# An inverse transform on half-height PE tiles, and a new written-out order, in a two-layer kernel on one core

## The chip, the cores and the metric

The kernel runs on one core of a Trainium2 chip. A core has TensorE (PE, matmuls, writes to PSUM), VectorE (DVE), ScalarE (ACT), GpSimd (POOL) and SyncE (SP, which here only issues DMAs), each with its own instruction queue, worked off in order; they meet through semaphores. The metric is the device time of one execution in microseconds, the median of several runs.

## The reference

The sequence has 2,048 positions of 512 channels, bf16. Two layers, each a mixer and an MLP, and each preceded by a layer norm:

```python
k_shift = sum of four taps of k over time     # a short filter per channel
kv  = k_shift * v
y   = irfft(rfft(kv, 4096) * rfft(ssm_k, 4096))[:2048] + kv * ssm_D
x   = x + layernorm(x) * y                    # q of the mixer is the normed x
h   = gelu(layernorm(layernorm(x)) @ w1 + b1) # 512 -> 1376
x   = x + h @ w2 + b2                         # 1376 -> 512
```

`y` depends on k, v and the filter alone, not on x: it is computed once and used by both layers. The norm before the MLP is followed by the MLP's own, so it is taken twice in a row. The long convolution (`y`) and the two MLPs are nearly all of the work.

## The kernel before, in words

The sequence is treated in two halves of 1,024 positions (half 0, half 1), each transformed by a two-step Fourier transform written as matmuls:

- `turn`, `shift_turn`: transposes of the filter `ssm_k` and of k on PE. `shift`, `shift_pair`: the four-tap filter as matmuls, `shift` with 64-row tiles (line 610), `shift_pair` with 32-row tiles (line 638); VectorE multiplies by v (lines 616 and 647).
- `stage1` (line 553, tags h1 for the filter and x1 for kv): 128 points, on PE tiles of 128 rows by 64 columns.
- `stage2` (line 565, tags h2, x2): eight points by the table S2, 16 matmuls of 64 columns to a tile. The result has channels, frequencies and real or imaginary part mixed over the partitions.
- `swap`: DMAs from SBUF to SBUF that exchange real and imaginary rows, so that VectorE can multiply the two spectra (line 464).
- `inverse1` (line 665, tags i1_0 and i1_1) and `inverse2` (line 683, i2_0, i2_1): back again. `inverse1` works on eight tiles `j` of eight channel groups `i`; each has two matmuls `n` (two addends) with the spectrum as weights, read at a stride of four elements, and 128 columns of the table U. All of a spectrum must be there before its first tile. `evac` (lines 469 on ScalarE and 470 on VectorE) takes the tile out of PSUM.

The products of half 1 are formed by the multiplies of tag x2_1 and the adds of tag sum (VectorE, lines 777 and 779); i1_1 reads them.

Around this run the MLPs: 13 blocks of 128 to 512 positions, nine of half 0 (both layers) and four of half 1. A block is statistics and norms on VectorE, GpSimd (the power for the reciprocal root) and ScalarE, a transposing DMA (line 866), the matmuls m1 (line 886) with gelu on ScalarE (line 891), and m2 (line 920), cut in pieces of 4, 4 and 3 matmuls of 512 columns, with the residual add on VectorE (line 924). Blocks of half 0 fill PE while half 1 is transformed.

The order is written out by hand of a planner: all 1,185 operations are numbered as the program text makes them, and `SEQ` lists the numbers. Each engine's queue is the sublist that falls to it. `ENGS` chooses the engine of every operation that has a choice (a, v, p for ACT, DVE, POOL), `BANKS` the PSUM bank of every tile. Waits follow from the data. Numbers that matter here: 4 to 7 loads of the filter, 8 to 11 of k, 12 to 15 of v, 16 to 31 of S2, 133 to 136 of the filter's second half, 195 to 198 of q; 356 to 371 i1_1 (even a PE tile, odd its eviction), 372 to 385 i2_1; 682, 735 to 737 and 739 pieces of m2; 898 on, the first block of half 1.

```python
o.eng = o.engs[0] if len(o.engs) == 1 else {"a": ACT, "v": DVE, "p": POOL}[next(choice)]
```

Of the kernel before, what the change touches and what calls it, by code (L numbers as in the profile page):

```python
# [36 lines left out]
class Prog:  # L37
# [60 lines left out]
    ENGS = ("apvpvvvpavaavaaaaaavvvaaavvvpvpvaavaaaaavaavvaaaaaaaavavaaaaaavaaavaaaaaappppaaaaaaaaaaaaaaaaaaaaaaaaaaaaapvvp"  # L98
            "paappvppaappvvvpaappaappaappaappaappaappvavpaappvappaappvvppvvvpaappvvavvvvvvavpvvvvppavavpvvvvvpvaaavpvvaaapv"
            "avva")  # L100
    BANKS = ("02220326464004602026041320002442462264542202240064064646402046462667062260046446220462640604660406064226644472"
             "44450442172316353547502206314500451400554567076567013226140174645320543403764701436154766316307007062272260403"
# [243 lines left out]
def _tables():  # L346
# [10 lines left out]
    S2 = np.zeros((2, 8, 8, 128, 2, 8, 8))  # L357
# [603 lines left out]
```

## Time and profile before

| | |
|---|---|
| median of 3 runs | 239.22 us (239.12 to 239.52) |
| span of the profiled execution | 238.6 us; its time with what lies around the span is not listed apart |
| PE busy | 226.9 us, 95% |
| VectorE busy | 178.1 us, 75% |
| ScalarE busy | 159.6 us, 67% |
| GpSimd busy | 55.3 us, 23% |
| mean granted PE clock | 0.993 |
| moved by DMA | 26.75 MB, most of it before 60 us |

In a row of the profile, L665 is line 665 of the kernel. A group's row gives shapes, the count, after the bar the busy time and the mean duration of one in ns, and then the engine's idle time just before them with what ended it. Matmuls overlap in the pipe: their durations (some 219 ns for 128 columns) are much longer than the distance between two starts, so costs on PE are read from starts. The timeline merges neighbours of one kind and shows the start, the length and the count.

### The profile page before, as it was taken

What the parts mean: (1) busy time and instruction counts of PE and PEld (TensorE: products, weight loads), DVE (VectorE), ACT (ScalarE), POOL (GpSimd) and SP (SyncE); (2) the same over time, 40 slices, a digit from 0 to 9 for tenths busy, and PEclk for the clock granted to TensorE, in tenths of its full rate; (3) what the DMA queues carried; (4) which work ended last, traced back from release to release, by engine and by line L of the source; (5) the groups of instructions that cost most, each with busy time, mean ns of one, the idle gap of its engine ahead of it and who ended that gap; (6) DMA issues with size and microseconds to landing.
All of it is one profiled execution on the core that took longest, in us unless ns stands there. A gap on an engine that the chain in (4) does not pass through costs nothing.

```text
span 238.6 us, 6251 instructions
## 1 busy us (share of the span) xinstructions
PE 226.9 (95%) x2615; PEld 152.3 (64%) x2637; DVE 178.1 (75%) x358; ACT 159.6 (67%) x255; POOL 55.3 (23%) x120
## 2 busy tenths in 40 slices
PE   6998698899999999999999999999999999999995
PEld 3897588885968588667769675644445444444454
DVE  0579869999999999999999999593579469404013
ACT  2586879999996899999768786359036606831630
POOL 2421030104623506446004522303020210200000
PEclk9999979999999999999999999999999999999999
DMA  6999767989946660053100304200300050132202
GB/s 173 350 393 388 272 181 186 257 267 194 163 87 197 153 140 3 1 69 103 54 0 15 80 0 83 49 3 12 78 0 3 18 157 0 25 66 91 84 0 91
DMA packets 41112, 26.75 MB, mean 112 GB/s; under 512 B 23702, under 2 KB 33788, under 8 KB 41084
## 3 DMA queue, kind: packets, MB, share of 16 engines
q1 hardware_dynamic: 40786, 26.20, 40.5%
q8 instruction: 21, 0.34, 0.6%
q10 hardware_dynamic: 298, 0.16, 0.3%
q14 instruction: 7, 0.06, 0.1%
HBM read 15.07 MB, written 2.10 MB: 72 GB/s over the span
## 4 chain that ended last, share of the span: by engine, by line
PE 83%; DVE 6%; DMA 4%; ACT 3%; issue 2%; POOL 1%; SPq 1%; POOLq 0%
PE ps L886 32%; PE ps L920 31%; PE ps L665 6%; PE ps L553 5%; PE ps L565 3%; ACT ar L469 3%; DMA ar<-in_A_ssm_k_dram 2%; DVE ar L464 2%; DMA ar<-ar 2%; DVE ar L616 1%; PE ps L683 1%; PE ps L909 1%; PE ps L638 1%; PE ps L610 1%; DVE ar L470 1%
## 5 line engine op out<-in xcount | busy, mean ns | idle before, releaser
L891 ACT ACTIVATE ar<-ps,sm 128x256 bf16<-128x256 f32 (+4 forms) x143 | 65.4, 525 | 41.0 <-PE ps L886 39.5
L469 ACT ACTIVATE ar<-ps 128x1024 bf16<-128x1024 f32 (+3 forms) x77 | 71.3, 1005 | 16.4 <-PE ps L553 6.4
L886 PE MATMUL ps<-ar 128*128 128x256 bf16 (+4 forms) x568 | 81.5, 297 | 0.3
L920 PE MATMUL ps<-ar 128*128 128x512 bf16 (+1 forms) x324 | 77.2, 379 | 1.1 <-issue 0.3
L886 PEld LDWEIGHTS ps<-ar 128*128 128x128 bf16 (+1 forms) x572 | 52.8, 100 | 28.1 <-ACT ar L891 0.4
L464 DVE TENSOR_TENSOR ar<-ar 128x512 bf16<-128x512 bf16 (+3 forms) x105 | 62.7, 637 | 0.9 <-ACT ar L469 0.4
L920 PEld LDWEIGHTS ps<-ar 128*128 128x128 bf16 (+1 forms) x341 | 32.4, 98 | 33.4 <-ACT ar L891 0.2
L924 DVE TENSOR_TENSOR ar<-ar,ps 128x512 bf16<-128x512 bf16 x31 | 20.7, 678 | 33.2 <-PE ps L920 33.0
L797 DVE BATCH_NORM_STATS2 sm<-ar 128x6 f32<-128x512 bf16 x64 | 42.9, 683 | 0.5
L822 ACT ACTIVATE ar<-ar,sm 128x512 bf16<-128x512 bf16 x34 | 26.4, 811 | 9.5 <-DVE sm L809 8.3
L804 POOL TENSOR_TENSOR sm<-sm 128x2 f32<-128x2 f32 (+2 forms) x26 | 23.6, 909 | 23.8 <-DVE sm L802 22.0
L802 POOL TENSOR_SCALAR sm<-sm 128x2 f32<-128x2 f32 (+2 forms) x21 | 6.4, 304 | 97.3 <-DVE sm L798 97.1
L553 PE MATMUL ps<-ar 128*64 128x128 bf16 x512 | 18.6, 227 | 3.1 <-issue 1.4
L565 PEld LDWEIGHTS ps<-ar 128*128 128x128 bf16 x512 | 18.4, 102 | 3.4 <-ACT ar L469 1.0
L565 PE MATMUL ps<-ar 128*128 128x64 bf16 x512 | 19.6, 199 | 0.5 <-ACT ar L469 0.4
L553 PEld LDWEIGHTS ps<-ar 128*64 128x64 bf16 x512 | 15.7, 114 | 6.1 <-issue 2.6
L812 POOL TENSOR_SCALAR sm<-sm 128x1 f32<-128x1 f32 x43 | 16.1, 390 | 2.0
L470 DVE CAST ar<-ps 128x1024 bf16<-128x1024 f32 x11 | 13.3, 1222 | 4.3 <-PE ps L565 2.8
L665 PE MATMUL ps<-ar 128*128 128x128 bf16 x256 | 15.0, 219 | 0.5 <-DVE ar L464 0.4
L665 PEld LDWEIGHTS ps<-ar 128*128 128x128 bf16 x256 | 14.7, 113 | 1.2 <-DVE ar L464 0.6
L823 DVE TENSOR_SCALAR ar<-ar,sm 128x512 bf16<-128x512 bf16 x30 | 11.8, 410 | 3.4 <-POOL sm L812 3.1
L470 DVE COPY ar<-ps 128x1024 bf16<-128x1024 bf16 (+1 forms) x9 | 5.5, 632 | 8.0 <-PE ps L516 5.3
(41 smaller groups left out, 94.3 us busy)
## 6 DMA issues: line engine op xcount, KB each, us to landing
ar<-tab_s SPq DMA_DIRECT2D x16, 256.0 KB, 9.0
ar<-ar SPq DMA_DIRECT2D x16, 256.0 KB, 3.7
ar<-in_A_ssm_k_dram SPq DMA_DIRECT2D x8, 256.0 KB, 6.8
ar<-in_A_q_dram SPq DMA_DIRECT2D x8, 256.0 KB, 4.7
ar<-in_A_v_dram SPq DMA_DIRECT2D x8, 256.0 KB, 6.1
out_dram<-ar SPq DMA_DIRECT2D x7, 256.0 KB, 2.5
ar<-in_B_w_dram SPq DMA_DIRECT2D x4, 344.0 KB, 4.8
ar<-in_B_w_dram SPq DMA_DIRECT2D x5, 256.0 KB, 4.0
```

Source lines behind the costliest of these rows:

```text
L464: return P.op(eng, lambda e: e.tensor_tensor(o, a, b, op), dur, reads=[a, b] + list(more), writes=[o])
L469: return e.activation(dst, src(), AF.Copy)
L470: return e.tensor_copy(dst, src())
L553: r = e.matmul(Q(tl, 64 * ri, 64, i * 128, [1, 128]), w, m, start=True, stop=True)
L565: r = e.matmul(Q(tl, 0, 128, i // 8 * 512 + i % 8 * 4, [32, 16], [1, 4]), w, m, start=True, stop=True)
L665: r = e.matmul(Q(tl, 0, 128, i * 128, [1, 128]), w, m, start=n == 0, stop=n == 1)
L797: P.op(DVE, lambda e, sj=sj, x=x: e.bn_stats(sj, x), 600.0, reads=[x], writes=[sj])
L804: P.op(POOL, lambda e: e.tensor_tensor(r, v, hf, ALU.pow), 420.0 + 149.0 * n, reads=[v, hf], writes=[r])
L822: return e.activation(o, x, AF.Identity, bias=u, scale=r)
L886: r = e.matmul(Q(tl, 0, rows, 0, [1, w]), a, m, start=dk == 0, stop=dk == 3)
L891: P.op(ACT, lambda e, dst=dst, tl=tl, rows=rows, bias=bias, w=w: e.activation(dst, Q(tl, 0, rows, 0, [1, w]), AF.Gelu_apprx_tanh, bias=bia ...
L920: r = e.matmul(Q(tl, 0, 128, 0, [1, 512]), ins[fc][0], ins[fc][1], start=fc == 0, stop=fc == 10)
```

## The change

The output columns of S2 change places: channel `d` of a group of eight moves from the middle of the partition index to its front, even channels first. So partitions 0 to 63 hold the even channels of a group and 64 to 127 the odd ones. The rows of U follow. For half 1 `inverse1` uses this: in place of a matmul over 128 rows and 128 columns it issues two, one on rows 0 to 63 for the even channels and one on rows 64 to 127 for the odd ones, each with 64 columns of U at a step of two elements, the two into different PSUM banks. The eviction then writes with a step of two. i1_0 stays as it is.

Further, `SEQ`, `ENGS` and `BANKS` are replaced as a whole. Of the operations with a choice, 32 go to VectorE from elsewhere and 26 leave it. On PE, i1_1 was one tile, three matmuls of m2 and then seven tiles; it is now four tiles, seven matmuls of m2, four tiles. All eight of its evictions are on ScalarE in both.

```diff
     SEQ = (
-        33, 34, 6, 214, 1, 44, 0, 35, 36, 4, 7, 2, 39, 51, 3, 38, 11, 52, 8, 41, 9, 10, 45, 5, 195, 15, 12, 54, 46, 13, 53,
...
-        766, 800, 723, 802, 764, 730, 717, 731, 857, 858, 679, 685, 724, 862, 803, 718, 861, 859, 713, 714, 681, 686, 366,
-        722, 682, 732, 368, 863, 804, 367, 805, 864, 865, 866, 364, 806, 369, 360, 767, 809, 365, 810, 361, 358, 359, 765,
-        356, 357, 362, 370, 807, 811, 735, 808, 363, 812, 371, 683, 867, 813, 736, 374, 372, 737, 373, 873, 376, 868, 738,
...
+        42, 0, 6, 43, 214, 1, 4, 33, 2, 5, 34, 41, 7, 3, 195, 9, 11, 10, 8, 196, 51, 14, 197, 45, 52, 12, 209, 46, 35,
...
+        731, 343, 681, 732, 751, 684, 355, 720, 754, 685, 752, 799, 686, 755, 368, 753, 800, 687, 358, 369, 757, 360,
+        359, 801, 366, 855, 756, 735, 367, 802, 758, 856, 803, 804, 682, 361, 759, 370, 760, 862, 761, 356, 762, 371,
+        858, 364, 857, 763, 860, 357, 362, 805, 766, 736, 806, 363, 767, 861, 764, 863, 859, 739, 807, 365, 864, 808,
...
-    S2 = S2.transpose(0, 1, 2, 3, 5, 6, 4).reshape(128, 128 * 128)
+    S2 = S2[..., [0, 2, 4, 6, 1, 3, 5, 7]].transpose(0, 1, 2, 3, 6, 5, 4).reshape(128, 128 * 128)
...
-    U = U.transpose(1, 2, 0, 3, 4, 5, 6).reshape(128, 256)
+    U = U[:, :, [0, 2, 4, 6, 1, 3, 5, 7]].transpose(2, 1, 0, 3, 4, 5, 6).reshape(128, 256)
...
-    def inverse1(p, q, Z):
+    def inverse1(p, q, Z, split):
...
-                    ins.append((i, n, A(0, 128, r + (dg // 4) * 512 + dg % 4, [4, 128]), A(0, 128, R_U + n * 128, [1, 128])))
+                    o = r + (dg // 4) * 512 + dg % 4
+                    if split:
+                        for g in range(2):
+                            ins.append((512 * g + 4 * i, n, A(64 * g, 64, o, [4, 128]), A(64 * g, 64, R_U + n * 128 + g, [8, 16], [2, 4])))
+                    else:
+                        ins.append((i * 128, n, A(0, 128, o, [4, 128]), A(0, 128, R_U + n * 128, [1, 128])))
...
-                    r = e.matmul(Q(tl, 0, 128, i * 128, [1, 128]), w, m, start=n == 0, stop=n == 1)
+                    r = e.matmul(Q(tl, 0, 128, i, *([32, 16], [1, 4]) if split else ([1, 128],)), w, m, start=n == 0, stop=n == 1)
                 return r
-            P.op(PE, f, 16 * 56.0, reads=[x for y in ins for x in y[2:]], tile=tl)
+            P.op(PE, f, 32 * 18.0 if split else 16 * 56.0, reads=[x for y in ins for x in y[2:]], tile=tl)
+            if split:
+                evac(BOTH, A(0, 128, Z + 64 * j, [1, 2], [512, 16], [2, 32]),
+                     lambda tl=tl: Q(tl, 0, 128, 0, [512, 2], [32, 16], [1, 32]), E1, tl)
+                continue
...
-    inverse1(R_1, R_2, R_3)
+    inverse1(R_1, R_2, R_3, False)
...
-    inverse1(HH, HI, R_Z1)
+    inverse1(HH, HI, R_Z1, True)
```

More of the change, by code (lines that the diff above doesn't have):

```diff
@@ L44 @@
     SEQ = (
[53 rows of a table removed]
[L98 to L102, printed above, removed]
-             "71655156407602371631706316706615043246755274432051240747516203416017010")
[55 rows of a table added]
+    ENGS = (
+            "avapapvpaavvaavaavaaaaavvvvapvppvavvavaavaavvaaaaaaaavaaaaaaaaavaavaaaaaapvpvaaaaaaaaaaaaaaaaaaaaaaaaaaa"
+            "aappappaavpvppaappvvppaapvaappaappaappaappaappavppvappaapvaappvvppvappvapvvvaapvavavvvvavvvvvvvvpvvvvvvv"
+            "aavvpvaavvvvavvv")
+    BANKS = (
+            "45704306202464200000627236026646246464226006402420624644066042640262264660244620204426464644246204266020"
+            "22247020226337626301520172570440464475725755436672367720371021321620440063513741720454430362521124671007"
+            "27743140661373223714364027332203342000120556367705202105351567170234501404453107474")
     def __init__(self, nc):
```

100 rows, old and new, of the table SEQ are left out of this document.

## The prediction

> **What bounds the kernel now.** I read the page's busy shares first.
>
> ```profile
> span 238.6 us, 6251 instructions
> ...
> PE 226.9 (95%) x2615; PEld 152.3 (64%) x2637; DVE 178.1 (75%) x358; ACT 159.6 (67%) x255; POOL 55.3 (23%) x120
> ```
>
> TensorE (PE) is the bound, but a share of the span mixes stages. So the second view is the busy time in stretches: after each stretch stand its length, then PE, weight load (PEld), DVE, ACT, POOL, granted clock, DMA share and GB/s.
>
> ```profile
> 60.00:125.00 65.00, 64.18 (x909) 48.38 (x920) 64.40 (x112) 56.62 (x113) 24.14 (x41) 1.00 0.41 89
> 125.00:147.00 22.00, 21.89 (x218) 15.99 (x218) 21.23 (x59) 17.80 (x27) 8.51 (x19) 1.00 0.17 38
> 147.00:236.00 89.00, 88.53 (x448) 43.93 (x454) 46.17 (x113) 39.28 (x66) 9.48 (x20) 1.00 0.17 44
> ```
>
> From 60 us to the end PE hardly stops: 174.60 of 176 us. There a microsecond less of PE work is a microsecond of the result, provided that what PE waits for keeps up. What can fail to is VectorE (DVE): from 60 to 125 us it too is busy, 64.40 of 65.
>
> The changed stage is the second half's first inverse: line 665 on PE, line 469 its evictions. Third come the chain of waits in order of time (start, length) and the timelines of PE, ScalarE and VectorE.
>
> ```profile
> 124.95 0.90 PE ps L665 x16
> ...
> 126.49 6.26 PE ps L665 x112
> ```
> ```profile
> 124.78 1.06 PE L665 MATMUL ps<-ar 128*128 128x128 bf16 x16
> ```
> ```profile
> 127.43 6.52 ACT L469 ACTIVATE ar<-ps 128x1024 bf16<-128x1024 f32 x7 [0.52 <-PE ps L665]
> ```
> ```profile
> 111.96 12.78 DVE L464 TENSOR_TENSOR ar<-ar 128x2048 bf16<-128x2048 bf16 x14
> ```
>
> The stage starts on PE at 124.78, as VectorE ends the sums that it reads (111.96 + 12.78 = 124.74). Two busy engines meet there with no slack.
>
> **The change, part by part.** *PE work of i1_1.* Removed are 128 matmuls, 0.90 + 6.26 = 7.16 us, 55.9 ns each. Added are 256 matmuls of 64 rows and 64 columns, in 128 pairs of an upper and a lower row tile. The rows that bound the price of a pair, from PE's timeline, the chain and the groups by shape:
>
> ```profile
> 15.76 2.82 PE L610 MATMUL ps<-ar 64*128 64x256 bf16 x66
> ...
> 20.16 1.05 PE L610 MATMUL ps<-ar 64*128 64x256 bf16 x22
> ```
> ```profile
> 105.01 0.47 PE ps L565 x16
> ```
> ```profile
> 72.05 1.11 PE L638 MATMUL ps<-ar 32*128 32x128 bf16 x88
> 73.10 4.54 PE L886 MATMUL ps<-ar 128*128 128x256 bf16 x40
> ```
> ```profile
> L886 PEld LDWEIGHTS ps<-ar 128*128 128x128 bf16 x520 | 47.4, 98 | 26.1 <-ACT ar L891 0.4 <-ACT ar L469 0.3
> ...
> L665 PEld LDWEIGHTS ps<-ar 128*128 128x128 bf16 x256 | 14.7, 113 | 1.2 <-DVE ar L464 0.6 <-issue 0.2
> ```
>
> Line 610 runs 64-row tiles already: 44 more matmuls take 2.82 - 1.05 = 1.77 us, 40.2 ns each, though they stream 186 columns on average (22 matmuls of one filter stream 4,096, counted in the code). At line 665's 55.9 ns for 128, 186 columns take 81 ns alone, so the two halves run side by side. A full matmul with 64 columns takes 0.47 / 16 = 29.2 ns (line 565, unit-stride weights). That is a pair's low end: 128 x 29.2 = 3.74 us. The new weights are read at a stride of four elements, as line 665's are now, and such a load lasts 113 ns against 98 for unit stride, 15 ns more. Since a unit-stride load hides within 29.2, a strided one needs at most about 44: 128 x 44 = 5.63 us. I take the middle, 36.6, as neither row is nearer: 4.68 us, a gain of **2.48** (1.53 to 3.42).
>
> A rule speaks against this. The Trainium skill, "TensorE: Matmul & The Clock Gate", section "Wait — 56ns, not 53.3ns?", says that start-to-start never drops below about 25 ns, however few the columns. Held for every matmul, it gives 256 x 25 = 6.4 us and a gain of 0.76 instead of 2.48, an estimate from that page. The trace does not agree where neighbours are on different row tiles: line 638 issues 88 between 72.05 and 73.10, 11.9 ns each.
>
> *Mode changes.* The work around i1_1 uses the whole array. PE's timeline around a column-tiled stage shows what a change of tiling costs:
>
> ```profile
> 87.54 0.64 PE L553 MATMUL ps<-ar 128*64 128x128 bf16 x16
> 88.11 2.79 PE L886 MATMUL ps<-ar 128*128 128x256 bf16 x24
> 90.83 1.53 PE L553 MATMUL ps<-ar 128*64 128x128 bf16 x48
> 92.29 2.38 PE L886 MATMUL ps<-ar 128*96 128x256 bf16 x20
> ```
>
> From start to next start, 16 take 0.57 us and 48 take 1.46: 27.8 ns each and 0.125 left over for the change back. I take 0.1 per change, for either direction. Counted in the two orders from the first MLP tile on, there are 11 changes before and 17 after: four more from i1_1, which comes in two groups of four tiles, two from x1_1, cut into more pieces. **+0.6** (0.4 to 0.75).
>
> *Evictions of i1_1.* Still eight, all on ScalarE, 6.52 / 7 = 0.93 us each; their write is now strided by two elements. Line 469's minimum, median and maximum, over evictions of many layouts:
>
> ```profile
> L469 ACT ACTIVATE ar<-ps x77: 575/1023/1166, 7.2 to 144.3; 128x1024 bf16<-128x1024 f32 x67, 128x1024 bf16<-128x1024 bf16 x4, 128x512 bf16<-128x512 f32 x4, 128x512 bf16<-128x512 bf16 x2
> ```
>
> The layout hardly shows, so I take 0. The cover: from the first i1_1 to the first i2_1 the new order gives PE 4.68 + 0.4 + five pieces of m2 (18 matmuls of 512 columns; at four times line 665's 55.9 or less, up to 4.0), some 9.0 us; ScalarE needs one tile of 0.6 and 8 x 0.93, so 8.0. An eviction may slow by 0.12 us before PE waits; past that, all eight count.
>
> *Tables.* The same bytes in another column order; stage 2 and i1_0 keep their shapes: 0.
>
> *The order, late.* Up to the last sum VectorE's new list has two more evictions of 1024 elements, two fewer transpose copies, two fewer multiplies and one norm fewer (both 512 wide, priced alike), one residual add more. Its timeline and the groups by shape price them:
>
> ```profile
> 10.46 2.35 DVE L470 CAST ar<-ps 128x1024 bf16<-128x1024 f32 x2 [1.15 <-PE ps L553]
> 13.07 1.29 DVE L470 COPY ar<-ps 128x1024 bf16<-128x1024 bf16 x2 [0.25 <-PE ps L536]
> ```
> ```profile
> L464 DVE TENSOR_TENSOR ar<-ar 128x512 bf16<-128x512 bf16 x64 | 25.2, 417 | 0.8 <-ACT ar L469 0.4
> ...
> L924 DVE TENSOR_TENSOR ar<-ar,ps 128x512 bf16<-128x512 bf16 x31 | 20.7, 678 | 33.2 <-PE ps L920 33.0
> ```
>
> With busy time over count (0.39 and 0.67) that is 2.35 - 1.29 - 3 x 0.39 + 0.67 = +0.56 us, ahead of a stage that VectorE releases. PE brings 0.2 of its own by then (x1_1's two mode changes), so up to 0.4 of waiting is new; VectorE's 0.6 us of idle between 60 and 125 may take it all. **+0.2** (0 to 0.4).
>
> Behind the sums comes the second half's first MLP block. Now VectorE's last norm for it and PE's arrival stand here:
>
> ```profile
> 146.94 0.39 DVE L823 TENSOR_SCALAR ar<-ar,sm 128x512 bf16<-128x512 bf16 x1
> ```
> ```profile
> 152.54 10.54 PE L886 MATMUL ps<-ar 128*128 128x256 bf16 x55
> ```
>
> VectorE's last norm ends 22.6 us after its last sum; its new list there is longer by about 1.9 (two multiplies, three statistics of some 0.67, aggregates, less one add): 24.5. The transposing load behind it takes about 3, so 27.5. PE reaches the block now 29.1 us after i1_1's start (152.54 and three last 256-wide tiles, 1.3), in the new order 29.1 - 2.48 + 0.4 + two more tiles of the half before, 0.9: 27.9. The wait is 0 by 0.4 us.
>
> *The order, early.* All four loads of the filter now lead, three of q come early, and the last load of v moves from the 13th place to the 17th on SyncE's queue. SyncE's timeline, the landing times of v, the stretch that gives the load rate, and v's first reader:
>
> ```profile
> 5.72 2.47 SPq L449 DMA_DIRECT2D ar<-in_A_v_dram  x4
> ```
> ```profile
> DMA to landing us min/median/max: 3.5/6.1/7.4
> ```
> ```profile
> 10.00:20.00 10.00, 9.56 (x244) 8.74 (x238) 7.76 (x10) 6.75 (x8) 1.87 (x5) 1.00 1.05 391
> ```
> ```profile
> 17.74 2.36 DVE L616 TENSOR_TENSOR ar<-ps,ar 128x1024 bf16<-128x1024 f32 x2 [1.53 <-PE ps L610]
> ```
>
> Four places of 256 KB at 391 GB/s are 2.7 us. The last v lands by 5.72 + 2.47 + 7.4 = 15.6 and its reader starts at 17.74, released by PE: 2.1 us of cover for 2.7, and VectorE has 0.9 us more other work queued ahead of that reader. I take **0**, between +2.3 and -2.5 (rivals two and three).
>
> **Sum:** -2.48 + 0.6 + 0.2 + 0 = -1.7 us, a span of 236.9. The profiled span of 238.6 lies 0.6 under the median run of 239.22, which holds what is around it; carried over: **237.5 us**.
>
> **Rivals.** *One, slower: the pace is per matmul.* If each 64-row matmul keeps line 565's 29.2 ns, i1_1 takes 256 x 29.2 = 7.48: 239.22 + 0.32 + 0.8 = 240.3. It decides above 25 ns per matmul (0.8 back from 7.16). Line 638's 11.9 speaks against it. *Two, slower: PE falls to half clock once more, early.* PE was idle before such a stretch:
>
> ```profile
> 28.20 1.42 issue
> ```
> ```profile
> 30.52 4.52 PE L565 MATMUL ps<-ar 128*128 128x64 bf16 x96
> ```
>
> 96 at 29.2 ns are 2.80 us; they took 4.52. The new order runs all of h1_0 ahead of the filters, so near 18 to 22 us PE has little but x1_0, and each of its tiles waits for a multiply of 1.18 us (line 616). One more such stretch costs 1.7, with the 0.6 by which v lacks cover 2.3: 239.8. It decides above 1.7. *Three, faster: the present stretch and stall vanish,* and the swap behind them starts earlier: 1.4 + 1.7 = 3.1 at most, some 2.5 kept: 235.0. *Four: the edit does not do what it says,* the two halves' strided loads take turns: 128 x 88 = 11.3 us in place of 7.16, 244.2. Line 638's pace speaks against it. *Five: the block behind i1_1 waits for VectorE's longer list* and the saving is given back: 239.2, for a slip of 2.1 us.
>
> **Chances.** Forecast 0.55 (its own range 236.4 to 238.8, by the ends above), two 0.20, three 0.15, one 0.05, four 0.03, five 0.02. A difference under 0.2% (0.5 us) can't be told from none. Faster is the forecast but for 0.01, and three: 0.69. Slower is one, four and 0.16 of two: 0.24. Within is the rest, 0.07. For 8 in 10 the range takes in two and three: 235.0 to 240.3.
>
> **What would show it.** Pairs of line 665's new form about 36 ns apart are right, 29 or 44 a size off, 58 or 88 rivals one and four. Further: i1_1 in two groups of some 2.4 us with changes of 0.1 around them, evictions still at 0.93, PE without gaps after 60 us, the first MLP tile near 60 us as now. It is wrong if that tile moves by over 1 us, if the clock dips a second time, or if PE waits for VectorE at i1_1 by over 0.5 us.

## The result, and the profile after

The changed kernel takes 240.13 us (median; 238.77 to 242.25), the kernel before, run beside it, 239.26: a ratio of 1.004, interval 1.0022 to 1.0058. It is slower by 0.4%, where 237.5 us and "faster" was forecast.

The head of the page of the changed kernel, and its busy time in stretches (columns as in the prediction: length, PE, PEld, DVE, ACT, POOL, granted clock, DMA share, GB/s):

```profile
span 238.0 us, 6496 instructions
...
PE 222.9 (94%) x2743; PEld 146.8 (62%) x2765; DVE 179.0 (75%) x364; ACT 161.2 (68%) x254; POOL 49.0 (21%) x104
```
```profile
60.00:125.00 65.00, 64.16 (x908) 47.17 (x917) 64.14 (x110) 55.84 (x112) 15.26 (x33) 1.00 0.43 91
125.00:147.00 22.00, 20.48 (x347) 13.62 (x345) 19.32 (x56) 21.14 (x29) 7.89 (x17) 1.00 0.13 26
147.00:236.00 89.00, 88.05 (x444) 43.62 (x450) 48.34 (x122) 37.22 (x63) 6.94 (x9) 1.00 0.20 47
```

PE's busy time fell by 4.0 us (226.9 to 222.9), 1.1 of which the profile of before owed to a stretch at half clock (below; label k, without it, has 225.8). The span hardly followed. In the stretch of the changed stage, 125 to 147 us, PE now waits 1.5 us and ScalarE is the busier engine, 21.14 of 22. The chain of waits there, PE's timeline and ScalarE's:

```profile
121.81 3.02 PE ps L933 x14
124.83 0.67 PE ps L674 x28
125.51 0.02 issue
125.53 9.59 ACT ar L473 x8
```
```profile
124.76 1.79 PE L674 MATMUL ps<-ar 64*128 64x64 bf16 x96
126.93 0.72 PE L674 MATMUL ps<-ar 64*128 64x64 bf16 x32 [0.38 <-ACT ar L473]
...
131.67 0.72 PE L674 MATMUL ps<-ar 64*128 64x64 bf16 x32 [0.47 <-ACT ar L473]
...
135.16 1.47 PE L696 MATMUL ps<-ar 128*128 128x512 bf16 x6 [0.29 <-ACT ar L473]
```
```profile
125.53 9.58 ACT L473 ACTIVATE ar<-ps 128x1024 bf16<-128x1024 f32 x8 [1.66 <-PE ps L674]
```

The chain, which was PE alone here, leaves PE after the first tile and runs through all eight evictions: 9.58 / 8 = 1.20 us each, 0.93 before. PE waits at the fourth tile, at the last, and at the second inverse. That is one place where the gain went.

The other lies ahead. Here are the largest waits of PE up to 60 us, and rows of its timeline there (start, length):

```profile
PE ps L511 <- POOL ar L505: 1.8, 1, 1.8
PE ps L614 <- DVE ar L620: 1.3, 1, 1.3
PE ps L569 <- ACT ar L473: 1.1, 3, 0.5
PE ps L557 <- POOL ar L468: 1.1, 1, 1.1
PE ps L557 <- ACT ar L473: 1.0, 1, 1.0
PE ps L887 <- ACT ar L835: 0.8, 1, 0.8
```
```profile
11.34 1.98 PE L557 MATMUL ps<-ar 128*64 128x128 bf16 x64 [1.07 <-POOL ar L468]
...
19.85 1.05 PE L614 MATMUL ps<-ar 64*128 64x256 bf16 x22 [1.33 <-DVE ar L620]
...
59.15 0.84 PE L899 MATMUL ps<-ar 128*128 128x128 bf16 x12 [0.22 <-ACT ar L473]
59.85 0.40 PE L887 MATMUL ps<-ar 128*128 128x128 bf16 x4
60.11 3.94 PE L899 MATMUL ps<-ar 128*128 128x128 bf16 x60
63.89 0.63 PE L569 MATMUL ps<-ar 128*128 128x64 bf16 x16
```

The first wait is the start of PE's work, 1.3 us in the kernel before. At 11.34 PE waits for a one-row add of the filter's transpose (line 468 on GpSimd); on GpSimd's queue two filter tables (line 527, 0.65 us each) stand ahead of it. At 19.85 the last 64-row filter tile waits for a multiply of VectorE (line 620). For comparison, the kernel before in a run without half clock, the same places and the two ends of the part behind (label k below; lines 553, 565, 610, 886, 665 and 909 are 557, 569, 614, 899, 674 and 922 after):

```profile
19.18 1.08 PE L553 MATMUL ps<-ar 128*64 128x128 bf16 x32 [0.43 <-DVE ar L616]
20.32 1.05 PE L610 MATMUL ps<-ar 64*128 64x256 bf16 x22
...
29.66 3.23 PE L565 MATMUL ps<-ar 128*128 128x64 bf16 x96
...
58.38 3.97 PE L886 MATMUL ps<-ar 128*128 128x128 bf16 x68
62.18 0.63 PE L565 MATMUL ps<-ar 128*128 128x64 bf16 x16
...
122.77 1.06 PE L665 MATMUL ps<-ar 128*128 128x128 bf16 x16
...
232.18 1.99 PE L909 MATMUL ps<-ar 128*128 128x256 bf16 x22
```

Before, tiles of another stage (line 553) fill PE ahead of the last filter tile. i1_1 starts at 122.77 there, at 124.76 in the changed kernel: 2.0 us lost ahead of the stage that was to bring the gain.

### The profile page after: what moved, and what is told of

The parts are those of the page before. It is cut to its first block, busy times and chain, and to the rows that moved or that the text cites. A ratio compares the mean times of both kernels' runs of the same rounds, so it can differ in the third digit from the quotient of the medians.

```text
span 238.0 us, 6496 instructions
## 1 busy us (share of the span) xinstructions
PE 222.9 (94%) x2743; PEld 146.8 (62%) x2765; DVE 179.0 (75%) x364; ACT 161.2 (68%) x254; POOL 49.0 (21%) x104
## 4 chain that ended last, share of the span: by engine, by line
PE 76%; ACT 11%; DVE 7%; issue 3%; POOL 1%; POOLq 0%
PE ps L899 31%; PE ps L933 29%; ACT ar L473 9%; PE ps L569 4%; DVE ar L468 4%; PE ps L557 3%; PE ps L696 2%; DVE ar L474 2%; PE ps L614 2%; DVE ar L620 2%; PE ps L674 1%; PE ps L511 1%; ACT ar L904 1%; PE ps L922 1%; PE ps L642 1%
## 5 line engine op out<-in xcount | busy, mean ns | idle before, releaser
L904 ACT ACTIVATE ar<-ps,sm 128x256 bf16<-128x256 f32 (+5 forms) x143 | 65.8, 523 | 37.3 <-PE ps L899 37.1
L473 ACT ACTIVATE ar<-ps 128x1024 bf16<-128x1024 f32 (+3 forms) x77 | 73.8, 1038 | 14.0 <-PE ps L557 5.5
L899 PE MATMUL ps<-ar 128*128 128x256 bf16 (+5 forms) x568 | 81.9, 297 | 0.5 <-ACT ar L473 0.2
L817 POOL TENSOR_TENSOR sm<-sm 128x2 f32<-128x2 f32 (+2 forms) x26 | 21.4, 822 | 32.3 <-DVE sm L815 30.5
L569 PEld LDWEIGHTS ps<-ar 128*128 128x128 bf16 x512 | 16.6, 98 | 3.6 <-ACT ar L473 1.5
L474 DVE CAST ar<-ps 128x1024 bf16<-128x1024 f32 x13 | 15.8, 1219 | 2.4 <-PE ps L569 1.5
L674 PE MATMUL ps<-ar 64*128 64x64 bf16 (+1 forms) x384 | 12.8, 203 | 1.2 <-ACT ar L473 1.1
L674 PEld LDWEIGHTS ps<-ar 64*128 64x128 bf16 (+1 forms) x384 | 11.9, 114 | 2.8 <-ACT ar L473 2.0
L767 DVE SCALAR_TENSOR_TENSOR ar<-ar,sm,ps 128x512 bf16<-128x512 bf16 x16 | 10.7, 741 | 0.4 <-PE ps L569 0.4
L811 DVE BATCH_NORM_AGGREGATE sm<-sm 128x2 f32<-128x6 f32 x64 | 10.1, 171 | 0.6
```

What stands on the lines that cost most here:

```text
L473: return e.activation(dst, src(), AF.Copy)
L474: return e.tensor_copy(dst, src())
L569: r = e.matmul(Q(tl, 0, 128, i // 8 * 512 + i % 8 * 4, [32, 16], [1, 4]), w, m, start=True, stop=True)
L674: r = e.matmul(Q(tl, 0, 128, i, *([32, 16], [1, 4]) if split else ([1, 128],)), w, m, start=n == 0, stop=n == 1)
L817: P.op(POOL, lambda e: e.tensor_tensor(r, v, hf, ALU.pow), 420.0 + 149.0 * n, reads=[v, hf], writes=[r])
L899: r = e.matmul(Q(tl, 0, rows, 0, [1, w]), a, m, start=dk == 0, stop=dk == 3)
```

## The experiments

i1_1 cuts the kernel in two: its first matmul, and the time from there to the last matmul of the kernel, both from PE's timeline. The second number is steady to some hundredths of a microsecond; the first carries the arrival of loads and the clock of that run. The kernel before was run beside each of the others, with medians of 238.74 to 239.26 us; the ratios are to those, so times of different rows are best compared by them. "Rows" is the edit with 64-row tiles, "step" its eviction writing at a step of two.

| kernel | order | i1_1 | first i1_1 (us) | i1_1 to last matmul (us) | time (us) | ratio to before (interval) |
|---|---|---|---|---|---|---|
| before (k, l) | before | full array | 122.77, 122.80 | 111.40 | 238.37, 238.49 (one run each) | |
| after | new | rows, step | 124.76 | 110.78 | 240.13 | 1.0040 (1.0022 to 1.0058) |
| a | before | full array | 124.41 | 111.40 | 239.39 | 1.0014 (0.9988 to 1.0039) |
| b | before | rows, step | 124.02 | 112.53 | 241.19 | 1.0108 (1.0068 to 1.0149) |
| c | new | full array | 125.85 | 111.39 | 241.30 | 1.0109 (1.0070 to 1.0148) |
| d | new | rows, plain write, PSUM step | 124.67 | 112.75 | 242.93 | 1.0185 (1.0151 to 1.0218) |
| e | new | rows, plain write, banks in turns | 124.68 | 109.36 | 238.26 | 0.9986 (0.9956 to 1.0015) |
| g | before | as e | 124.41 | 110.64 | 238.53 | 0.9990 (0.9965 to 1.0014) |
| h | before, then new | as after | 128.81 | 110.75 | 244.78 | 1.0253 (1.0208 to 1.0298) |
| i | new, then before | full array | 125.61 | 111.40 | 240.82 | 1.0080 (1.0048 to 1.0112) |
| j | before, then new | as e | 133.92 | 109.34 | 247.82 | 1.0365 (1.0320 to 1.0411) |
| m | before, moved at i1_1 | as e | 123.26 | 115.28 | 243.05 | 1.0173 (1.0124 to 1.0222) |

**The edit and the order apart (a, b, c).** a is the kernel before itself. b is the changed kernel with the lists of before:

```diff
     SEQ = (
-        42, 0, 6, 43, 214, 1, 4, 33, 2, 5, 34, 41, 7, 3, 195, 9, 11, 10, 8, 196, 51, 14, 197, 45, 52, 12, 209, 46, 35,
+        33, 34, 6, 214, 1, 44, 0, 35, 36, 4, 7, 2, 39, 51, 3, 38, 11, 52, 8, 41, 9, 10, 45, 5, 195, 15, 12, 54, 46, 13, 53,
...
```

c is the new order without the edit of i1_1:

```diff
-    inverse1(HH, HI, R_Z1, True)
+    inverse1(HH, HI, R_Z1, False)
```

> The kernel before, unchanged, against itself: what a second profile of it shows. The one profile of it so far had a clock of 0.993 and a stretch at half clock near 31 us; the changed kernel's runs show 1.0. If that stretch is a feature of the order, it is there again (clock about 0.993, span 238 to 239). If it is an accident of one run, the clock is 1.0 and the span 237 to 238, about 1 us less, and the base of my sum was an untypical run. Ratio of the times 0.998 to 1.002.

> The edit alone: parity tables and the split first inverse, with the order, engines and banks of before. Theory one (the strided eviction: 9.59 us for eight on ScalarE, 1.20 each, in place of 0.93, sets the stage): i1_1 takes PE some 4.3 us instead of 7.16, but eight evictions need 9.6, the first i2_1 comes later than before by 0.5 to 1 us, PE waits 1.5 to 3 us there, and the time is within 0.5 us of before or up to 1 us over it. Rival (the new order is to blame, the edit is good): faster than before by 1.5 to 2.5 us.

> The order alone: order, engines, banks and tables of the changed kernel, i1_1 unsplit (128 rows, 128 columns, eviction in runs of eight elements as before). Theory one: evictions are back at 0.93 us, PE does 2.9 us more in i1_1 but loses the 1.5 us of waiting and 0.4 of mode changes there, so about 1 us slower than the changed kernel, 240.5 to 241.5. Rival (the order is to blame): the same or slower than that as well, so this run does not decide between them alone; with the run of the edit alone it gives the order's own cost: under theory one over 1 us against before, under the rival too. If it is faster than the changed kernel, the split as such loses.

Against itself the kernel before came out even. Either part alone costs 1.1%; together they cost 0.4%. PE's timeline of b at i1_1:

```profile
127.62 0.72 PE L670 MATMUL ps<-ar 64*128 64x64 bf16 x32 [0.20 <-ACT ar L469]
128.79 0.71 PE L670 MATMUL ps<-ar 64*128 64x64 bf16 x32 [0.45 <-ACT ar L469]
129.98 0.72 PE L670 MATMUL ps<-ar 64*128 64x64 bf16 x32 [0.48 <-ACT ar L469]
...
134.66 1.04 PE L692 MATMUL ps<-ar 128*128 128x512 bf16 x4 [0.41 <-ACT ar L469]
```

In the order of before the tiles follow one another with no other work between. Their starts then lie 1.17 to 1.19 us apart, the length of an eviction: the faster matmuls only lengthen the wait. From i1_1 on b needs 112.53 - 111.40 = 1.1 us more than before. The run is slower by more, 2.2 us by the medians, which is more than either expectation; 1.25 us of it stand in its profile ahead of i1_1 (124.02 against 122.77, same lists), as a later table load and longer "issue" waits of PE. Whether they belong to that run or to the longer program stays open.

c shows where the order costs. From i1_1 on it needs 111.39 us, the kernel before 111.40: nothing is lost or won there. Its whole loss lies ahead of i1_1, at 125.85. That is 1.1 us later than in the three other profiles of this order (124.67 to 124.76), so c's 1.1% overstates the order's own cost. And c beside the changed kernel says that even with its slow evictions the edit pays in the new order, 111.39 - 110.78 = 0.6 us, because the new order puts m2 between the tiles.

**Is it the step of two in the eviction's write? (d, e)** Both write whole runs. d writes the parities as two runs of 32 and lets the second inverse put them in place as it writes PSUM:

```diff
-                evac(BOTH, A(0, 128, Z + 64 * j, [1, 2], [512, 16], [2, 32]),
+                evac(BOTH, A(0, 128, Z + 64 * j, [32, 2], [512, 16], [1, 32]),
...
-                    r = e.matmul(Q(tl, 0, 128, al * 512, [1, 512]), a, m, start=ri == 0, stop=ri == 1)
+                    r = e.matmul(Q(tl, 0, 128, al * 512, *([64, 8], [1, 2], [2, 32]) if split else ([1, 512],)), a, m, start=ri == 0, stop=ri == 1)
```

e writes runs of 64 and reads PSUM in turns from the two banks instead:

```diff
-                evac(BOTH, A(0, 128, Z + 64 * j, [1, 2], [512, 16], [2, 32]),
-                     lambda tl=tl: Q(tl, 0, 128, 0, [512, 2], [32, 16], [1, 32]), E1, tl)
+                evac(BOTH, A(0, 128, Z + 64 * j, [512, 16], [1, 64]),
+                     lambda tl=tl: Q(tl, 0, 128, 0, [32, 16], [1, 32], [512, 2]), E1, tl)
```

> The changed kernel with the step of two moved out of the eviction: ScalarE writes even and odd channels in two runs of 32, and the second inverse of this half sorts them where PE writes PSUM (a step of two floats). Theory one: evictions of i1_1 fall from 1.20 to about 0.93 us, the stage from the first i1_1 to the first i2_1 from 10.4 to about 8.8 us, PE's waits there from 1.5 to under 0.3, and the time by 1 to 2 us against the changed kernel: 238.1 to 239.1. It falls short if PE's write at a step of two is slow: the 30 matmuls of i2_1 then last more than 216 ns from start to start. Rival (strided writes are not what costs; ScalarE is slow there for another reason, such as PSUM banks shared with PE): evictions stay at 1.15 or more and the time within 0.4 us of the changed kernel.

> The changed kernel, but each eviction of the second half's first inverse writes runs of 64 channels and takes the parities apart on the reading side (PSUM read in turns from two banks). Theory one (it is the step of two in the bfloat16 write that made the eviction 1.20 us instead of 0.93): evictions of 0.90 to 0.97 us, the stage from its first matmul to the second inverse 8.2 to 8.6 us instead of 10.40, the second inverse at 216 ns a matmul, and the run 1.5 to 2.1 us below the changed kernel: 238.0 to 238.6, ratio to before 0.995 to 0.998. Rival (reading two banks in turns costs what the write cost): evictions of about 1.2 us and a ratio of 1.004 as the changed kernel has. Third (the block behind is bound by VectorE or ScalarE): evictions 0.93, but the first matmul of the 512-wide part of the block 29.2 to 29.8 us after the stage's start as before, ratio 1.002 to 1.004.

d, ScalarE's timeline and then PE's:

```profile
125.43 3.78 ACT L473 ACTIVATE ar<-ps 128x1024 bf16<-128x1024 f32 x4 [1.66 <-PE ps L674]
129.53 3.78 ACT L473 ACTIVATE ar<-ps 128x1024 bf16<-128x1024 f32 x4 [0.33 <-PE ps L674]
```
```profile
128.78 2.56 PE L674 MATMUL ps<-ar 64*128 64x64 bf16 x128
...
133.66 2.74 PE L696 MATMUL ps<-ar 128*128 128x512 bf16 x6
```

The evictions are back at 3.78 / 4 = 0.945 us and PE no longer waits at the tiles: the step in the write was the cause. But now six matmuls of the second inverse last 2.74 us where they took 1.47 in the changed kernel, 0.21 us more each, and d is the slowest of the whole orders. e has the first without the second; ScalarE's timeline and PE's:

```profile
125.45 3.78 ACT L473 ACTIVATE ar<-ps 128x1024 bf16<-128x1024 f32 x4 [1.66 <-PE ps L674]
129.56 3.78 ACT L473 ACTIVATE ar<-ps 128x1024 bf16<-128x1024 f32 x4 [0.34 <-PE ps L674]
```
```profile
124.68 2.57 PE L674 MATMUL ps<-ar 64*128 64x64 bf16 x128
127.18 1.69 PE L933 MATMUL ps<-ar 128*128 128x512 bf16 x7
128.80 2.56 PE L674 MATMUL ps<-ar 64*128 64x64 bf16 x128
131.29 2.55 PE L933 MATMUL ps<-ar 128*128 128x512 bf16 x11
133.69 1.46 PE L696 MATMUL ps<-ar 128*128 128x512 bf16 x6
...
232.06 1.98 PE L922 MATMUL ps<-ar 128*128 128x256 bf16 x22
```

Two groups of four tiles, 2.50 us each from their start to that of the next work (127.18 - 124.68), with m2 between and no wait marked. The stage takes 9.0 us (133.69 - 124.68) and not the 8.2 to 8.6 expected: PE's own work fills it now. From i1_1 on e needs 109.36 us: 1.4 less than the changed kernel and 2.0 less than c. The run is 1.9 us below the changed kernel by the medians, 1.3 by the ratios. Against the kernel before it is even: 0.9986, an interval on both sides of 1.

**The same eviction in the order of before (g).**

b's lists and e's eviction together.

> The kernel before with its order, engines and banks, the row-tile matmuls, and the eviction that reads the banks in turns. Theory one (edit good, eviction bad): the stage to the second inverse is bound by eight evictions of 0.93 us behind a first tile of 0.53 to 0.58: 8.2 to 8.6 us instead of 9.53 before, so 0.9 to 1.3 us faster than before, ratio 0.9945 to 0.9965. Rival (the evictions cost 1.2 us on the reading side too): as the edit on the old order measured, ratio 1.011. Third (the gain is taken back behind the stage): ratio 0.998 to 1.002.

```profile
125.82 2.56 PE L674 MATMUL ps<-ar 64*128 64x64 bf16 x128
128.57 0.72 PE L674 MATMUL ps<-ar 64*128 64x64 bf16 x32 [0.19 <-ACT ar L473]
129.49 0.72 PE L674 MATMUL ps<-ar 64*128 64x64 bf16 x32 [0.20 <-ACT ar L473]
130.41 0.72 PE L674 MATMUL ps<-ar 64*128 64x64 bf16 x32 [0.20 <-ACT ar L473]
```

In PE's timeline of g the tiles now come 0.92 us apart, bound by the evictions still. From i1_1 on that is 111.40 - 110.64 = 0.8 us better than before, a little under what was expected. The run, 0.999, can't be told from none and so lies where the third theory put it, but not for its reason: the stage itself gains 0.8 (8.75 us, 133.16 - 124.41, for 9.52 in k, 132.29 - 122.77), and nothing of that is given back behind it. What hides it lies ahead of i1_1, 124.41 against 122.77 in k. In the new order the same edit is worth 2.0 (c to e), since the cover between its tiles lets PE's whole gain through.

**Where ahead of i1_1 (k, l, h, i).** k and l are the kernel before, for profiles without half clock. h has the first 314 operations (to the first MLP tile) in the order of before and goes on in the new one; i is the counterpart, 308 new ones and then the order of before, with full-array matmuls in i1_1. The joint of h against the order of before, and that of i against the new one:

```diff
-        259, 481, 484, 204, 485, 487, 486, 403, 410, 445, 411, 488,
+        259, 481, 484, 204, 485, 487, 486, 403, 302, 301, 294, 208,
```
```diff
-        401, 441, 243, 284, 442, 402, 291, 244, 257, 584, 403, 585,
+        401, 441, 243, 284, 442, 402, 291, 244, 213, 387, 443, 257,
...
-    inverse1(HH, HI, R_Z1, True)
+    inverse1(HH, HI, R_Z1, False)
```

> The kernel before once more, for a profile at the full granted clock. Theory one (the new order loses ahead of the second half's first inverse): at full clock the inverse starts at 122.9 to 123.7 us, against 124.7 to 125.9 in the four profiles of the new order. Rival (no loss there): 124.3 us or later.

> The same as the look before it, a second draw: the clock fell to half for a stretch in about half of the runs of this order. Theory one at full clock: start of the second half's first inverse at 122.9 to 123.7 us; at half clock for a stretch up to 1.5 us later. Rival: 124.3 us or later at full clock.

> The counterpart: the first 308 operations in the new order, the rest in the order of before, with full-array matmuls in the second half's first inverse (new tables and layouts). Theory one (loss in the early part): ratio 1.004 to 1.006. Rival (early part even): ratio 0.999 to 1.001.

> The changed kernel, but up to the first matmul of the first block's first layer (the first 314 operations) the order, engines and banks of before. Theory one (the new order loses 1.0 to 1.4 us in its first 60 us): 1.0 to 1.4 us below the changed kernel, ratio 0.998 to 1.000. Rival (the loss of the new order lies in the stretch from the first block to the second half's first inverse, 65.6 us instead of 64.4): ratio 1.003 to 1.005, as the changed kernel.

k and l start i1_1 at 122.77 and 122.80, 0.1 below theory one's bounds and far from the rival's. i points the same way: 111.40 from i1_1 on, exactly before's, and its start at 125.61 carries all of its 0.8%. That is more than either expectation, and i is no clean counterpart: 0.8 us of it is a wait of PE for a load of weights (in_B_w) at 69.05, behind the joint, which no whole order has.

h told nothing on the question and met neither expectation. Behind the joint PE stands for 2.5 us on VectorE, a wait that neither whole order has:

```profile
PE ps L899 <- DVE ar L767: 2.5, 1, 2.5
```

One more thing differs by the early order. The row of the granted clock in the page's 40 slices, first the kernel before in run a, then the changed kernel:

```profile
PEclk9689999999999999999999999999999999999999
```
```profile
PEclk9999999999999999999999999999999999999999
```

Of the nine profiles whose first part is in the order of before, six have such a stretch (before, a, g, h, j, m; not b, k, l), at changing places; of the five in the new order (after, c, d, e, i) none has. The mean clocks on record for single runs say the same less sharply: they are below 0.999 in 34 of 64 runs of the kernel before, and in 6 of 44 in the new order (after, c, d, e). In the kernel before the median of those 34 runs is 239.19 us, that of the other 30 is 238.55: some 0.6 us. Its profile in the prediction began i1_1 2.0 us later than k (124.78); 1.3 of that are the 96 matmuls in 4.52 us where k has 3.23, and 1.1 a longer "issue" wait just ahead of them (1.42 against 0.34), which the clock is not shown to have caused; k loses 0.4 in other places. What sets the stretch off is open.

**A better version? (j, m)** j joins the orders later, after 690 operations at about 105 us, with e's eviction. m keeps the order of before and moves work at i1_1 only:

```diff
-        679, 685, 724, 862, 803, 718, 861, 859, 713, 714, 681, 686, 366, 722, 682, 732, 368, 863, 804, 367, 805, 864,
-        865, 866, 364, 806, 369, 360, 767, 809, 365, 810, 361, 358, 359, 765, 356, 357, 362, 370, 807, 811, 735, 808,
-        363, 812, 371, 683, 867, 813, 736, 374, 372, 737, 373, 873, 376, 868, 738, 814, 869, 870, 375, 774, 385, 815,
+        679, 685, 724, 862, 803, 718, 861, 859, 713, 714, 681, 686, 366, 722, 368, 687, 367, 682, 732, 863, 804, 805,
+        364, 369, 360, 864, 865, 866, 806, 358, 683, 735, 767, 365, 809, 356, 361, 810, 765, 362, 359, 807, 736, 811,
+        370, 357, 808, 737, 363, 812, 371, 738, 813, 867, 374, 372, 373, 873, 376, 868, 814, 869, 870, 375, 774, 385,
```

In j the joint reads, where the order of before went on with 662, 733, 799, 672:

```diff
-        677, 664, 633, 665, 674, 801, 760, 726, 662, 733, 799, 672,
+        677, 664, 633, 665, 674, 801, 760, 726, 675, 672, 673, 678,
```

> The first 690 operations (to about 105 us) in the order of before, the rest in the new order, with the row-tile matmuls and the evictions that read the banks in turns. Theory one (the new order loses its 1 to 2 us ahead of the second half's first inverse and nothing behind it, and its interleaving of that inverse with the block is what makes the row tiles pay): from the inverse's first matmul to the last matmul 109.4 us, as in the changed kernel with the same evictions, behind the first part of before: 236.6 to 237.6, ratio 0.990 to 0.996. Rival (a junction of two orders costs a stall, as the one at the first block did, or the new order's loss goes with its second part): ratio 0.998 or more, with more than 1 us of PE idle between 60 us and the inverse.

> The order of before with the row-tile matmuls and the evictions that read the banks in turns, and in the stretch of the second half's first inverse alone eleven second-layer matmuls (2.4 us of PE) drawn between its eight tiles and three ahead of the second inverse, in banks that two residual adds, drawn forward on VectorE, set free. Theory one (the eight evictions of 0.91 us on ScalarE bound this stretch, and work for PE between the tiles is what a row-tile edit needs; the order of before is 2 us better ahead of it): no PE wait of 0.2 us at the tiles, from the inverse's first matmul to the 512-wide part of the block 27.8 to 28.2 us instead of 28.73 without the moves and 29.5 before; 236.9 to 238.0, ratio 0.992 to 0.997. Rival (the residual adds drawn forward make VectorE late for the tokens of the next block, and PE waits there): the same as or more than without the moves, ratio 0.999 or above.

Behind i1_1, j gives what was expected, 109.34 us. Ahead of it the joint costs far more than the order saved, in one wait of PE (its list of waits, 60 to 140 us):

```profile
PE ps L899 <- DVE ar L937: 7.2, 1, 7.2
```

m met its rival. The two residual adds drawn forward (line 937) came only at 129.96 and 130.92 on VectorE, which is behind there with statistics and norms (PE had ended the first of the two sums of products by 123.3); the m2 that needed their PSUM bank waited (VectorE's timeline, then PE's waits):

```profile
129.96 0.66 DVE L937 TENSOR_TENSOR ar<-ar,ps 128x512 bf16<-128x512 bf16 x1
...
130.92 0.68 DVE L937 TENSOR_TENSOR ar<-ar,ps 128x512 bf16<-128x512 bf16 x1
```
```profile
PE ps L933 <- DVE sm L811: 3.6, 1, 3.6
```

So no version shown beats the kernel before by more than can be told.

## Why the prediction was wrong, step by step

Forecast was a change of -1.7 us. From k to the changed kernel, both at full clock, the spans differ by 238.0 - 236.6 = +1.4, and the terms add up to it:

| term of the sum | forecast (us) | measured (us) | from |
|---|---|---|---|
| PE work of i1_1 with its mode changes (one of the four falls ahead of its first matmul, in the last row) | -2.48 + 0.4 | -2.03 | c to e, from i1_1 on: 111.39 to 109.36 |
| evictions of i1_1 | 0 | +1.42 | e to after, from i1_1 on: 109.36 to 110.78 |
| the order behind i1_1 | 0 | 0 | k to c, from i1_1 on: 111.40 to 111.39 |
| the order ahead, x1_1's mode changes and VectorE's longer list in it | 0 + 0.2 + 0.2 | +1.99 | first i1_1, k to after: 122.77 to 124.76 |

- **PE work and mode changes: right, the size with some luck.** Four tiles, 64 pairs, take 2.50 us up to the start of the next work, which takes in the change back; 64 x 36.6 ns and one change of 0.1 make 2.44. The rows bounded a pair at 29 and 44 ns only, and the middle was taken for want of a nearer row. The change into the tiles falls ahead of i1_1: from the first MLP tile to i1_1 b needs 124.02 - 59.53 = 64.49 us, k 64.39, in the same order. Per matmul the four tiles make 2.50 / 128 = 19.5 ns. The rule set against this step stands in the Trainium skill's page "TensorE: Matmul & The Clock Gate", section "Wait — 56ns, not 53.3ns?": no less than some 25 ns from start to start. It does not hold here, where neighbours lie on different row tiles. Rivals one and four fall with the same number.
- **Evictions of i1_1: the step that failed first.** "The layout hardly shows, so I take 0" was drawn from a group's minimum, median and maximum over many layouts, none of which wrote at a step of two. It measured 1.20 us in place of 0.93. The reckoning of the cover held: PE's work from the first i1_1 to the first i2_1 takes 9.0 us in e, as forecast, and ScalarE needs 0.77 + 9.58 = 10.35 in the changed kernel, so 8 x 0.27 = 2.2 us on ScalarE came out as 1.4 of PE waiting. Whether waiting begins at 0.12 us for each, no run shows. What was missing was a range for a layout that no row showed.
- **The order, early: the step that failed by more.** It was set to 0 with a range of -2.5 to +2.3. Of the +2.0, some 1.7 are its own (0.2 are x1_1's mode changes, 0.1 is i1_1's first), which lies inside. Of the 2.0, 0.8 is there at the first MLP tile (58.38 to 59.15). The other 1.2 comes between that tile and i1_1: 65.6 us in the changed kernel, d and e, and 66.3 in c, against 64.4 to 64.5 where the order of before runs unbroken. It is pace and not work: a and e, whose traces have every matmul, have the same numbers of each kind there, but for four transposes of the norm. Those (59.85, line 887) stood ahead of the first tile before and take 0.26. Some 0.45 are lost at once, in the first block's m1: 72 matmuls take 0.70 + 3.78 = 4.48 us (59.15 to 59.85, 60.11 to 63.89), 62 ns each, where 68 in k take 3.80, 56 each; the single gaps are too short for the lists of waits, so what PE waited for there stays open. The mode changes take the 0.3 named above, as forecast. The last 0.15 or so lie in small steps. What sets the 0.8 ahead of the first tile is read from the waits shown above, and no run took one of them away.
- **Rival two** named the place, filter tiles that wait for VectorE's multiplies near 18 to 22 us (the 1.33 at 19.85), and the size, 2.3. Its mechanism, a second drop to half clock, did not come: the new order has fewer of them. v was not late either: VectorE's first multiply by v, at 18.56, waits for PE's filter tile (1.77 us) and for no load. So that the time came out near rival two's 239.8 was chance.
- **The order, late, and the block behind i1_1: right, within the range.** The 0.2 for VectorE did not come: its last sum ends at 117.81 + 6.10 = 123.91 in the changed kernel, and PE comes to i1_1 at 124.76 from m2, without a wait. Behind i1_1, 0 was right. **Rival three**, in which stall and half clock vanish and 2.5 us are won, was half right on the clock. It gained nothing in the end.
- **The base.** The span was taken to lie 0.6 under its run's time. The changed kernel's profiled run took 239.76 with a span of 238.0, k 238.37 with 236.6: 1.8 each. So the profile of before was of a run near 240.4, held up by the half clock and the wait ahead of it. Carrying the difference over to the median was sound, but a stretch that the median run partly lacks was counted as part of the kernel. The medians differ by 0.9 and not by 1.4, as the kernel before often pays for half clock and the changed one seldom does: at full clock the changed kernel's 18 runs have a median of 239.97, 1.4 over the 238.55 of the kernel before, though these were not run side by side.

## What to carry to other kernels

When an edit speeds up one engine's part of a stage, look at what the next engine must now do with the new layout: if no row of the trace shows that access pattern, give it a range, and put the step where it is free (here on the reading side of the eviction). A gain on PE in a stage that evictions bound is worth only as much as there is other work between its tiles. A new order is to be measured without the edit too; cut the kernel at one instruction and compare the part ahead with the part behind.

## What was not expected of the hardware

- An eviction of 128x1024 from fp32 to bf16 by ScalarE takes 1.20 us when its write steps by two elements, and 0.945 when the write is in runs of 32 or 64; to read PSUM in turns from two banks costs nothing that shows (e, 0.945). The write alone makes the difference: d and the changed kernel read PSUM alike. The Trainium skill's page "SBUF — State Buffer", section "Specifications (TRN2)", says in its row on cachelines that two hits in a line of 16 bytes are needed for full bandwidth; a step of two bf16 elements has four and would be free by it. For this write the measurement differs, and it decides.
- PE's write into PSUM at a step of two fp32 elements goes at half pace: of six matmuls of 512 columns each took 0.21 us more (2.74 against 1.47 us in all). The page "Advanced Engine Details and Errata" of the Trainium skill, section "PSUM Cachelines", says that two neighbouring fp32 elements should be written together; d agrees. The row tiles write PSUM in runs of four, and their 19.5 ns a matmul show no such loss against the forecast.
- The granted clock fell to half (0.50 from 31 to 34 us in the profile of before) for a stretch of the first 50 us in some profiles of one and the same kernel (before, a) and not in others (k, l); over 64 runs of it, 34 show a mean clock below 0.999.
